# Attention, gate and phase mixer on one core: an exponential written ahead of each series of sines, one buffer ring for it and the convolution's product, and token products that wait for token weights alone

## The chip, the cores and the metric

The kernel runs on one core of a Trainium2 chip. The metric is the device time of one execution in microseconds. Times inside an execution come from a profile of one execution: TensorE (PE, with its weight loads PEld), VectorE (DVE), ScalarE (ACT), GpSimd (POOL) and the DMA queues, whose issuer here is SyncE (SP).

## The reference

Three layers in a row on four batches of 576 tokens with 8 heads of 64, so 512 channels. Setup makes some weights double precision words, which the kernel converts itself.

```python
scores = scale * np.matmul(q, k.transpose(0, 1, 3, 2))
kth = np.partition(scores, -32, axis=-1)[..., -32:-31]     # the 32nd largest of each row
attn = softmax(where(scores >= kth, scores, -1e9)) @ v
...
gate = sigmoid(sum(conv_w[k] * xp[:, k:k + S, :] for k in range(5)))   # causal, per channel
x = (gate * (x @ w_val)) @ w_out
...
theta = x @ w_theta
y = einsum('ts,bsd->btd', w_tok_r, x * cos(theta)) + einsum('ts,bsd->btd', w_tok_i, x * sin(theta))
u = x + y
out = u + np.maximum(u @ w_ch, 0.0)
```

## The kernel before, in words

Attention is cut into 144 tiles of 128 query rows by 576 keys (two heads of 64 rows share the short last tiles). The main loop at the end of `mixer` makes one step per tile and works on many tiles at once, in a software pipeline: in step i it issues the scores of tile i+3 on TensorE (`scores_pe`), copies those of tile i+2 out of PSUM on ScalarE (`scores_out`), finds candidates among the scores of tile i on VectorE (`pick`), compares and counts on ScalarE and POOL (`count`, `below`), takes the threshold of tile i-4 (`rest`, L621), writes the exponential of tile i-5 on ScalarE (`expo`) and masks tile i-6 with it on VectorE (`mask`, L674). Behind that TensorE transposes the masked tile (`turn`), ScalarE copies the transposes to SBUF as pT (`turn_out`), and TensorE multiplies them with v (`close`, px). The order of these calls within a step is written out by hand in `STEP` (in the first half of the loop `SOON`). VectorE and ScalarE run their instructions in exactly the order in which they are written; the other engines' queues are ordered by the framework's scheduler, by the order of writing where buffers and data allow.

The two layers behind the attention are "jobs", Python generators in the list `jobs`: for each batch `front(b)` (value product pval, output product px2t, angles pth, sines, the mixed values z) and `back(b)` (token products py, channel products ph, transposes and stores). Each step `work` lets the first job write some products, until the step's allowance of 4,150 ns (`BASE`, in some stages 6,000) less the cost of the step's attention is spent. Only the first job in the list runs; one that yields "sync" ends the step's work. A job's follow-up instructions on other engines are put into lists: `mid` runs at a fixed place in the next step, `later` at one behind it. The front of batch b+1 is put into `jobs` when the last tile of that batch's attention is closed. Batch 0's front comes in two halves (token tiles 0 and 1, then 2, 3 and the short tile 4), as its attention does.

The weights come as double precision words and are converted piece by piece by `cvt` on ScalarE, VectorE and POOL, half a piece a step, in the order conv, val, out, theta, tok, ch. `lacking[name]` counts the pieces that are still to be written. `want` then splits a channel weight into a high and a low half (`halve`: ScalarE casts, VectorE subtracts) and stores the halves in DRAM; the buffers of these halves are those of the conversion's raw pieces.

ScalarE reads its functions from tables. Sines have a table of their own; `tabled` orders sines against the functions Exp and Tanh, so that they don't alternate more than they are written. `trig` writes a batch's sines and cosines in two series (in batches 1 and 2 both in one long step, in which a drain of the jobs writes all the angles; in batch 3 after the last exponential).

Buffers: the exponentials have two buffers (tag "e" of pool `wk`). The convolution's tap on ScalarE, `ct` (L834), which POOL adds to the gate (L835), has one (tag "ct"); two helpers of the fallback and of the final check use it as well. The kernel has a second, exact version behind a flag (`safe`), which isn't entered with these inputs.

Of the kernel before, what the change touches and what calls it, by code (L numbers as in the profile page):

```python
# [11 lines left out]
F32 = mybir.dt.float32  # L12
# [78 lines left out]
def mixer(ctx, tc, qT, kT, vt, w_val, conv_t, w_out, w_theta, w_tok, w_ch, out, flag):  # L91
    nc = tc.nc
    safe = flag is None
    P = 128
    B, S, DM = vt.shape
# [15 lines left out]
    LAG = G + FLAG  # L111
# [6 lines left out]
    wk = ctx.enter_context(tc.tile_pool(name="wk", bufs=1))  # L118
# [34 lines left out]
    N = len(seq)  # L153
# [37 lines left out]
    taken, lacking = set(), {}  # L191
# [216 lines left out]
    def halve(hi, lo, src, key, also=None):  # L408

        def higher():  # L410
            nc.scalar.copy(hi, src)
            later.append(lower)

        def lower():
            engine(key).tensor_tensor(lo, src, hi.bitcast(F32), ALU.subtract)
            if also is not None:
                also()
            if PATIENT and attending[0]:
                later.append(lambda: done.add(key))
            else:  # L420
                done.add(key)

        mid.append(higher)
# [20 lines left out]
    def place(k, m):  # L444

        if k < 3 or k % 3 == 2:
            dt = F32R if k < 3 else I32
            both = []
            for t in ("hi", "lo"):
                if (t, m) in (("lo", 0), ("lo", 1)):  # L450
                    both.append(ml.tile([P, DM], dt, tag=f"{t}{m}", name=f"{t}{m}_{k}"))
                    continue
                pair = f"{t}{m - m % 2}{m - m % 2 + 1}"
                if (pair, k) not in places:
                    places[pair, k] = ml.tile([P, 2, DM], dt, tag=pair, name=f"{pair}_{k}")
                both.append(places[pair, k][:, m % 2, :])
            return both
        if (k, 0) not in places:
            names = ("val", "out") if k % 3 == 0 else ("theta", "ch")
            for t in range(2):  # L460
                places[k, t] = cp.tile([P, NC, DM], I32, tag=f"w_{names[t]}", name=f"w{t}_{k}")
        return [places[k, t][:, m, :] for t in range(2)]
# [3 lines left out]
    def want(b, name, last=NC - 1):  # L466

        k = PHASES.index((b, name)) if b else -1
        if k > 2:
            return  # L470
        for m in range(last + 1):
            if (b, name, m) in mats:
                continue
            src = W[name][:, m, :] if name == "theta" else W[name][:, :, m * P : (m + 1) * P]
            both = place(k, m)
            mats[b, name, m] = both
            stored[name, m] = dp.tile([P, 2, DM], I32, name=f"{name}{m}")

            def store(both=both, to=stored[name, m]):
                for t in range(2):  # L480
                    nc.sync.dma_start(to[:, t, :], both[t].bitcast(I32))

            hi, lo = (t if name == "theta" else t.rearrange("p (c w) -> p c w", c=NC) for t in both)
            halve(hi, lo, src, ("w", b, name, m), store)
# [27 lines left out]
    def after(*keys):  # L512
        while not done.issuperset(keys):
            yield "sync"
# [108 lines left out]
    def thr(i):  # L623
        at = N - 1 - i + NK - 1
        return thrs[:, at : at + 1]

    def nmax(g):

        d = groups[g]
        nc.gpsimd.tensor_scalar(least[:, g * G : g * G + G, :], d["tops"][:, :, 0 : KC : KC - 1], -1.0 / SMALL, None,  # L630
                                ALU.mult)

    def one_by_one(g):

        d = groups[g]
        spare = wk.tile([P, S], F32, tag="ct", name=f"spare_{g}")
        for k in range(G):
            src = s_tiles[g * G + k]
            for r in range(K // 8):
                top = d["tops"][:, k, 8 * r : 8 * r + 8]  # L640
                nc.vector.max(top, src)
                if r < K // 8 - 1:
                    nc.vector.match_replace(spare, top, src, LOWEST)
                    src = spare
            nc.vector.tensor_copy(thr(g * G + k), d["tops"][:, k, K - 1 : K])
        nmax(g)

    def check():

        bad = cp.tile([P, 3], F32, name="bad")  # L650
        worse = wk.tile([P, S], F32, tag="ct", name="worse")[:, :N]
        for j, (what, limit, op) in enumerate(((thrs[:, NK - 1 :], 2.0 ** -90, ALU.is_le),
                                               (thrs[:, NK - 1 :], 0.5, ALU.is_ge),
                                               (least[:, :, 1], -2.0 ** -60, ALU.is_ge))):
            nc.vector.tensor_scalar(worse, what, limit, None, op)
            nc.vector.tensor_reduce(bad[:, j : j + 1], worse, mybir.AxisListType.X, ALU.add)

        def on_pe(spare):
            nc.tensor.matmul(spare[:1, :3], ones, bad, start=True, stop=True)
            return lambda: nc.scalar.activation(said, spare[:1, :3], AF.Copy, accum_out=flag)  # L660
        extras.append((3, on_pe))

    def expo(i):
        e = seq[i]
        e.exp = wk.tile([P, S], F32, tag="e", name=f"e_{i}", bufs=2)
        tabled(e.exp, s_tiles[i], AF.Exp, bias=least[:, i, 0:1], scale=1.0 / SMALL)

    def mask(i):
# [52 lines left out]
    def close(part):  # L721

        u, x = part["u"], part["x"]
        b, hp = divmod(u, NP)
# [49 lines left out]
        for c in range(NF + 1):  # L774
            for j in (1, 0):
                d = slice(64 * j, 64 * j + 64)
                of_v, k = (v[:, c, d], j * NF + c) if c < NF else (v_last[:, d], 2 * NF)
# [23 lines left out]
        if split and x:  # L801
            g = gate[b][hp]
        else:
            drain(("gate", (u - GB) // NP))
            g = sp.tile([P, S], F32, tag="gp", name=f"gp_{u}", bufs=GB)
# [3 lines left out]
        g = g[:, lo:hi]  # L809
# [20 lines left out]
            return  # L830
        nc.scalar.activation(g, taps[0], AF.Copy, scale=cw[:, hp, 0:1])
        for k in CT:
            ct = wk.tile([P, S], F32, tag="ct", name=f"ct_{u}_{x}_{k}")[:, : g.shape[1]]
            nc.scalar.activation(ct, taps[k], AF.Copy, scale=cw[:, hp, k : k + 1])  # L834
            nc.gpsimd.tensor_tensor(g, g, ct, ALU.add)  # L835
            yield
            yield
# [15 lines left out]
    def front(b, xs):  # L853
# [79 lines left out]
        def angle(i):  # L933

            if late and i == NF:
                return sin_of(b, i)
            return gv[i % NF][:, :DM] if three else sin_of(b, i)
# [29 lines left out]
                nc.scalar.activation(g, h, AF.Abs)  # L967

        def trig(which):
            for i in which:  # L970
                f = angle(i)
                if i < NF:
                    g = cos_of(b, i)
                    tabled(g, g, AF.Sin, bias=half_pi, scale=-TURN)
                    tabled(sin_of(b, i), f, AF.Sin, scale=-TURN)
                else:
                    tabled(sin_of(b, i), f, AF.Sin, bias=trig_bias, scale=-TURN)
            if NF in which:
                gate.pop(b)
                done.add(("gate", b))  # L980
            later.append(lambda: done.update(("trig", b, i) for i in which))
# [117 lines left out]
    def back(b):  # L1099
        x2T = ms.pop(b)  # L1100

        def y_out(m, h, ps):
            lo, hi = COLS[h]

            def f():
                nc.vector.tensor_tensor(x2T[:, m, lo:hi], ps, x2T[:, m, lo:hi], ALU.add)
                if m == NC - 1 and (h or b == B - 1):
                    for k in (h,) if b == B - 1 else range(2):
                        halve_room(b, k, "U", x2T)
                if not h and m % 2:  # L1110
                    want(b, "ch", m)
            return f

        while any(lacking.values()):
            yield "sync"
        if b < B - 1:
            for h, m in [(h, m) for h in range(2) for m in range(NC)]:
# [57 lines left out]
        def turned(tiles):  # L1175
            for i in tiles:
# [4 lines left out]
                later.append(store(i, w, po))  # L1181
                yield 450

        for h, m in [(h, m) for h in range(2) for m in range(NC)]:
            lo, hi = COLS[h]
            yield from after(*halved(b, h, "U"), ("w", b, "ch", m))
            ps = ps_m.tile([P, hi - lo], F32, tag="m", name=f"ph_{b}_{m}_{h}")
            yield from products(ps, [(mat(b, "ch", m, c), chunk(b, h, "U", c)) for c in range(NC)])
            later.append(h_out(m, h, ps))
            if (h, m) == (1, NC - 1):  # L1190
                used(b, "ch")
            yield paid()
            if h and m == 1:
                yield from after(*[("o", b, c, 0) for c in range(NC)])
                yield from turned([0, 1])
# [9 lines left out]
    for b in range(B):  # L1205
        late = b == B - 1
        f = 1.275 if b in THREE else 1.675
# [53 lines left out]
    for k, part in enumerate(order):  # L1261
        i0 = part["tiles"][0].i
        u, x = part["u"], part["x"]
# [5 lines left out]
        elif split or x == 0:  # L1269
            when = (i0 - 7, i0 - 5, i0 - 5, i0 - 4, i0 - 3) if split or i0 and order[k - 1]["x"] and order[k - 1]["u"] // NP in SPLIT else (i0 - 9, i0 - 8, i0 - 7, i0 - 6, i0 - 3)  # L1270
            a = (u, x if split else None)
            for step, do in zip(when, (load_heads, split_high, split_low, *(
                    lambda u, x, j=j: double(u, j, x) for j in range(2)))):
# [28 lines left out]
        now, later[:] = list(later), []  # L1302
        run(now)

    begun = [0.0]

    def inside(i, f):
        if 0 <= i < N:
            f(i)
# [50 lines left out]
        "loads": lambda i: run(at_step.pop(i, [])),  # L1360
    }
    for i in range(N + LAG + TO + 12):
        for name in SOON if i < N // 2 else STEP:
            DO[name](i)
    attending[0] = False
# [52 lines left out]
```

## Time and profile before

| | |
|---|---|
| median of 3 runs | 833.06 us (832.63 to 834.16) |
| the profiled execution | 829.74 us |
| its span, first to last instruction | 827.9 us |
| mean granted clock of TensorE | 0.958 |
| busy: PE, DVE, ACT, POOL | 725.3, 669.0, 634.0, 451.7 us |

A row of a timeline gives start, duration, engine, line, operation and tiles, and in brackets how long the engine stood idle before the instruction and which instruction ended that. L674 is line 674 of the kernel before. A row of the waits gives who waited for whom, then total, times and longest in us.

### The profile page before, as it was taken

The numbers are of one execution on the slowest core, as the hardware profiler recorded it, in microseconds if no ns is written. First come the engines' busy times: TensorE is split into PE (matmuls) and PEld (weight loads), VectorE is DVE, ScalarE is ACT, GpSimd is POOL, SyncE is SP. The second block draws the span as 40 slices with busy tenths as digits, with TensorE's granted clock in tenths as the row PEclk, the third lists the DMA queues.
The fourth block names the chain that finished last, engine by engine and source line by source line (L and its number), as shares of the span: only waits on it lengthen the run. The fifth ranks groups of instructions, "written<-read, shape, count | busy, mean of one in ns | idle before, by whom it ended". The sixth has DMA issues, their size and how long they took to land.

```text
span 827.9 us, 15411 instructions
## 1 busy us (share of the span) xinstructions
PE 725.3 (88%) x4478; PEld 584.6 (71%) x4478; DVE 669.0 (81%) x2708; ACT 634.0 (77%) x1517; POOL 451.7 (55%) x557
## 2 busy tenths in 40 slices
PE   5467799958995799989889989999999899999995
PEld 3346577635754586778778767778988777898895
DVE  5999999879976979799899979989998695363522
ACT  6788999889769768788988988889987785346511
POOL 5976777446644554546687625647896252005500
PEclk9998999979997699989998999999999999999998
DMA  5676776545342225234855543234763200071002
GB/s 151 167 186 168 197 175 171 136 110 139 97 133 47 71 81 145 53 83 135 230 170 160 163 133 86 46 85 126 189 172 109 103 7 10 1 223 39 2 1 62
DMA packets 69985, 94.33 MB, mean 114 GB/s; under 512 B 13315, under 2 KB 36739, under 8 KB 69891
## 3 DMA queue, kind: packets, MB, share of 16 engines
q1 hardware_dynamic: 69568, 92.82, 41.2%
q8 instruction: 38, 0.62, 0.3%
q14 instruction: 59, 0.46, 0.2%
q10 hardware_dynamic: 320, 0.43, 0.2%
HBM read 49.96 MB, written 13.11 MB: 76 GB/s over the span
## 4 chain that ended last, share of the span: by engine, by line
PE 47%; DVE 27%; ACT 15%; POOL 4%; issue 3%; DMA 2%; SPq 1%; ACTq 0%; POOLq 0%; DVEq 0%
PE py L1127 9%; PE px L778 8%; DVE cand L594 5%; PE ph L529 4%; DVE s L674 4%; DVE thrs L621 4%; PE px2t L529 4%; PE pval L529 4%; PE pth L529 4%; PE pt L687 3%; PE py L1146 3%; PE ps L558 3%; ACT n L607 2%; DVE cand L600 2%; DVE gp L843 2%
## 5 line engine op out<-in xcount | busy, mean ns | idle before, releaser
L615 POOL TENSOR_TENSOR y<-s,n 128x576 f32<-128x576 f32 x144 | 188.9, 1312 | 205.0 <-DVE thrs L621 144.0
L594 DVE MAX8 cand<-s 128x8 f32<-128x96 f32 x864 | 210.5, 244 | 0.8 <-ACT s L572 0.6
L674 DVE SCALAR_TENSOR_TENSOR s<-s,thrs,e 128x576 f32<-128x576 f32 x144 | 137.8, 957 | 10.9 <-ACT e L202 10.9
L607 ACT ACTIVATE n<-s,tops 128x576 bf16<-128x576 f32 x144 | 112.1, 778 | 32.3 <-POOL y L615 11.3
L572 ACT ACTIVATE s<-ps 128x256 f32<-128x256 f32 (+1 forms) x288 | 103.7, 406 | 33.5 <-PE ps L691 11.5
L1127 PE MATMUL py<-w_tok,z 128*128 128x256 f32 (+1 forms) x432 | 115.0, 407 | 3.4 <-DVE z L986 3.4
L687 PE MATMUL pt<-ident,s 128*128 128x128 f32 x576 | 95.8, 290 | 25.3 <-ACT pT L706 17.3
L621 DVE MAX8 thrs<-y 128x8 f32<-128x584 f32 x144 | 109.3, 759 | 4.1 <-POOL y L616 3.6
L202 ACT ACTIVATE e<-s,least 128x576 f32<-128x576 f32 x144 | 110.8, 769 | 0.5 <-DVE s L674 0.4
L687 PEld LDWEIGHTS pt<-ident,s 128*128 128x128 f32 x576 | 70.5, 148 | 49.9 <-ACT pT L706 21.9
L558 PE MATMUL ps<-kh_None,q 128*128 128x256 f32 x240 | 93.7, 397 | 5.9 <-ACT s L572 3.9
L1127 PEld LDWEIGHTS py<-w_tok,z 128*128 128x128 f32 x432 | 77.8, 190 | 22.3 <-DVE z L986 5.0
L706 ACT COPY pT<-pt 128x512 f32<-128x512 f32 x128 | 73.2, 572 | 25.8 <-PE pt L687 15.6
L778 PE MATMUL px<-pT,v 128*64 128x256 f32 (+1 forms) x512 | 75.3, 430 | 17.3 <-ACT pT L706 17.3
L598 DVE MAX8 tops<-cand 128x8 f32<-128x48 f32 x432 | 82.8, 192 | 0.1
L559 PE MATMUL ps<-kl_None,q 128*128 128x256 f32 x240 | 72.5, 305 | 0.0
L778 PEld LDWEIGHTS px<-pT,v 128*64 128x64 f32 x512 | 34.1, 142 | 47.2 <-ACT pT L706 19.7
L558 PEld LDWEIGHTS ps<-kh_None,q 128*128 128x128 f32 x240 | 47.4, 198 | 22.2 <-ACT s L572 10.7
L600 DVE MATCH_REPLACE8 cand<-tops,cand 128x48 f32<-128x48 f32 x288 | 55.2, 192 | 0.0
L558 PE MATMUL ps<-kh,q 128*128 128x256 f32 (+1 forms) x80 | 36.0, 458 | 21.4 <-ACT s L572 9.3
L559 PEld LDWEIGHTS ps<-kl_None,q 128*128 128x128 f32 x240 | 48.1, 200 | 2.7 <-issue 0.5
L695 ACT COPY pT<-ps 64x128 f32<-64x128 f32 (+1 forms) x160 | 39.2, 245 | 11.5 <-PE ps L691 5.6
(206 smaller groups left out, 1726.9 us busy)
## 6 DMA issues: line engine op xcount, KB each, us to landing
kh_None<-kh_None SPq DMA_DIRECT2D x48, 144.0 KB, 2.7
kl_None<-kl_None SPq DMA_DIRECT2D x48, 144.0 KB, 2.7
v<-in_vt_dram SPq DMA_DIRECT2D x20, 256.0 KB, 3.3
out_dram<-x2T SPq DMA_DIRECT2D x16, 256.0 KB, 3.0
w<-ch SPq DMA_DIRECT2D x16, 256.0 KB, 4.6
w<-theta SPq DMA_DIRECT2D x16, 256.0 KB, 5.4
raw_hi<-in_w_tok_dram SPq DMA_DIRECT2D x7, 512.0 KB, 4.0
kh<-kh SPq DMA_DIRECT2D x24, 144.0 KB, 2.4
```

Of the source, the lines that this page charges most:

```text
L202: ins = nc.scalar.activation(out, src, func, **more).ins
L529: nc.tensor.matmul(ps[o : o + n], x, y, start=(i + k == 0), stop=(i == last and k == len(ways) - 1), skip_group_check=(n < P))
L558: nc.tensor.matmul(bank[:, :w], q2, kh[:, lo:hi], start=(j == js[0]), stop=False)
L559: nc.tensor.matmul(bank[:, :w], q2, kl[:, lo:hi], start=False, stop=(j == js[-1]))
L594: nc.vector.max(d["cand"][:, k, 8 * x : 8 * x + 8], s_tiles[i][:, x * SUB : (x + 1) * SUB])
L607: nc.scalar.activation(n, s_tiles[i], AF.Sign, bias=d["tops"][:, k, KC - 1 : KC], scale=-(1.0 + 2.0 ** -22), accum_out=acc)
L615: nc.gpsimd.tensor_tensor(y[:, :S], s_tiles[i], d.pop(("n", k)), ALU.mult)
L621: nc.vector.max(thrs[:, N - 1 - i : N - 1 - i + NK], d.pop(("y", k)))
L674: nc.vector.scalar_tensor_tensor(p, p, thr(i), e.exp, ALU.is_ge, ALU.mult, accum_out=part["sums"][:, e.slot : e.slot + 1])
L687: nc.tensor.transpose(e.pt[:, c, :], p[:, c * P : (c + 1) * P], ident)
L778: nc.tensor.matmul(px[d, :], of_v, pT[:, k, :], start=(c == 0), stop=(c == NF), skip_group_check=True)
L1127: nc.tensor.matmul(ps, z[:, m * P : (m + 1) * P], W["tok"][:, w, lo:hi], start=(i + k == 0), stop=(i == NF))
```

## The change

Three edits. `expo` returns if the tile's exponential is already written, and `trig` calls it first, for the exponential that the next step would write (`step[0]` holds the loop's step). The tag "ct" is gone: the convolution's tap and the two helpers take buffers of tag "e", which now has three. `back` waits only for the token weights before the products py, and for the channel weights ahead of the products ph; the splits of channel weights that fall due before the last of these is converted are held in the list `due`.

```diff
@@ one_by_one, check: the same for spare and worse
-        spare = wk.tile([P, S], F32, tag="ct", name=f"spare_{g}")
+        spare = wk.tile([P, S], F32, tag="e", name=f"spare_{g}", bufs=3)
...
     def expo(i):
         e = seq[i]
-        e.exp = wk.tile([P, S], F32, tag="e", name=f"e_{i}", bufs=2)
+        if hasattr(e, "exp"):
+            return
+        e.exp = wk.tile([P, S], F32, tag="e", name=f"e_{i}", bufs=3)
         tabled(e.exp, s_tiles[i], AF.Exp, bias=least[:, i, 0:1], scale=1.0 / SMALL)
...
         for k in CT:
-            ct = wk.tile([P, S], F32, tag="ct", name=f"ct_{u}_{x}_{k}")[:, : g.shape[1]]
+            ct = wk.tile([P, S], F32, tag="e", name=f"ct_{u}_{x}_{k}", bufs=3)[:, : g.shape[1]]
...
         def trig(which):
+            if not safe:
+                inside(step[0] - LAG + 2, expo)
             for i in which:
...
-                if not h and m % 2:
-                    want(b, "ch", m)
+                if not h:
+                    due.append(m)
+                    while due and m % 2 and not lacking["ch"]:
+                        want(b, "ch", due.pop(0))
             return f

-        while any(lacking.values()):
+        due = []
+        while lacking["tok"]:
             yield "sync"
...
+        while lacking["ch"]:
+            yield "sync"
+        while due:
+            want(b, "ch", due.pop(0))
         for h, m in [(h, m) for h in range(2) for m in range(NC)]:
             lo, hi = COLS[h]
             yield from after(*halved(b, h, "U"), ("w", b, "ch", m))
...
-    begun = [0.0]
+    begun, step = [0.0], [0]
...
     for i in range(N + LAG + TO + 12):
+        step[0] = i
         for name in SOON if i < N // 2 else STEP:
```

## Rows read from the trace of the kernel before

**Rows 1.** The page, engines: busy us, share of the span, instructions.

```profile
PE 725.3 (88%) x4478; PEld 584.6 (71%) x4478; DVE 669.0 (81%) x2708; ACT 634.0 (77%) x1517; POOL 451.7 (55%) x557
```

**Rows 2.** VectorE's waits, whole span: us in total, times, longest.

```profile
DVE s L674 <- ACT e L202: 10.9, 3, 5.6
```

**Rows 3.** ScalarE's timeline, batch 0's second series of sines and after it.

```profile
255.06 1.28 ACT L202 ACT_TABLE_LOAD   x1
...
261.26 1.28 ACT L202 ACT_TABLE_LOAD   x1
262.56 0.77 ACT L202 ACTIVATE e<-s,least 128x576 f32<-128x576 f32 x1
263.24 0.57 ACT L706 COPY pT<-pt 128x512 f32<-128x512 f32 x1
...
277.75 0.76 ACT L202 ACTIVATE e<-s,least 128x576 f32<-128x576 f32 x1
```

**Rows 4.** VectorE's timeline in the same stretch.

```profile
257.41 0.40 DVE L340 TENSOR_SCALAR tmp<-tmp 128x512 f32<-128x512 f32 x1
263.37 0.82 DVE L674 SCALAR_TENSOR_TENSOR s<-s,thrs,e 128x576 f32<-128x576 f32 x1 [5.56 <-ACT e L202]
...
264.45 2.48 DVE L986 TENSOR_TENSOR z<-px,z 128x512 f32<-128x512 f32 x4
...
271.60 2.44 DVE L843 SCALAR_TENSOR_TENSOR gp<-xT,w_conv,gp 128x576 f32<-128x576 f32 x2
...
281.97 0.82 DVE L674 SCALAR_TENSOR_TENSOR s<-s,thrs,e 128x576 f32<-128x576 f32 x1
```

**Rows 5.** TensorE's timeline in the same stretch.

```profile
263.86 1.12 PE L687 MATMUL pt<-ident,s 128*128 128x128 f32 x4 [7.85 <-ACT pT L706]
...
286.25 4.05 PE L1127 MATMUL py<-w_tok,z 128*128 128x256 f32 x18
```

**Rows 6.** Instructions on tiles w_tok, w_ch: ns min/median/max, first to last start.

```profile
L354 POOL TENSOR_TENSOR w_tok<-raw_lo x4: 746/1492/1494, 145.2 to 229.6; 128x512 int32<-128x512 int32 x3, 128x64 int32<-128x64 int32 x1
...
L354 POOL TENSOR_TENSOR w_ch<-raw_hi x3: 1485/1487/1494, 242.6 to 282.2; 128x512 int32<-128x512 int32 x3
```

**Rows 7.** Stretches: length, busy PE, PEld, DVE, ACT, POOL; clock, DMA share, GB/s.

```profile
254.00:286.00 32.00, 17.32 (x87) 11.66 (x84) 26.41 (x101) 26.65 (x59) 18.03 (x20) 0.63 0.24 52
286.00:348.00 62.00, 59.99 (x347) 47.01 (x347) 52.71 (x243) 45.97 (x115) 29.90 (x37) 1.00 0.34 94
348.00:395.00 47.00, 40.96 (x286) 35.39 (x284) 44.56 (x183) 40.74 (x100) 28.72 (x36) 0.93 0.46 121
```

**Rows 8.** VectorE's waits from 286 to 395.

```profile
DVE x2T L1106 <- PE py L1127: 8.1, 4, 3.3
...
DVE x2T L1158 <- PE ph L529: 1.1, 1, 1.1
```

**Rows 9.** Groups by line: count, busy us, mean ns, idle before and its releaser.

```profile
L1127 PE MATMUL py<-w_tok,z 128*128 128x256 f32 (+1 forms) x432 | 115.0, 407 | 3.4 <-DVE z L986 3.4
...
L202 ACT ACT_TABLE_LOAD x9 | 11.5, 1283 | 0.2
```

**Rows 10.** POOL's timeline, batch 0's second series.

```profile
268.99 1.41 POOL L835 TENSOR_TENSOR gp<-gp,ct 128x576 f32<-128x576 f32 x1
```

**Rows 11.** Timelines of ScalarE and VectorE, batch 0's first series of sines.

```profile
172.64 0.42 ACT L202 ACTIVATE gp<-pconv 128x320 f32<-128x320 f32 x1
...
172.76 0.82 DVE L674 SCALAR_TENSOR_TENSOR s<-s,thrs,e 128x576 f32<-128x576 f32 x1 [4.48 <-ACT e L202]
```

**Rows 12.** Timelines of VectorE and TensorE, batch 1's sines and what follows.

```profile
479.17 0.69 DVE L950 SCALAR_TENSOR_TENSOR gp<-gp,pth 128x512 f32<-128x512 f32 x1 [4.10 <-ACT gp L943]
...
495.72 0.48 PE L1127 MATMUL py<-w_tok,z 128*128 128x256 f32 x1 [0.59 <-DVE z L986]
```

**Rows 13.** VectorE's timeline at 341.79; L621 alone from 286 to 348, busy, count.

```profile
341.79 0.49 DVE L1106 TENSOR_TENSOR x2T<-py,x2T 128x320 f32<-128x320 f32 x1 [3.34 <-PE py L1127]
...
286.00:348.00 62.00, 10.48 (x14) 1.00 0.34 94
```

More of the change, by code (lines that the diff above doesn't have):

```diff
@@ L650, in check @@
         bad = cp.tile([P, 3], F32, name="bad")
-        worse = wk.tile([P, S], F32, tag="ct", name="worse")[:, :N]
+        worse = wk.tile([P, S], F32, tag="e", name="worse", bufs=3)[:, :N]
         for j, (what, limit, op) in enumerate(((thrs[:, NK - 1 :], 2.0 ** -90, ALU.is_le),
```

## The prediction

> **What bounds the kernel now.** I read the page first: TensorE is busy 88% and VectorE 81% of the span [rows 1], so neither sets the time by its sum, and a change has to be read in its own stage. Then VectorE's waits over the whole span: the masking step (L674) waits only three times for ScalarE's exponential, 10.9 us in all [rows 2]. Then the timelines around the longest of these. In batch 0's second series of sines ScalarE loads the sine table at 255.06, loads the exponential's table at 261.26 and writes the next exponential at 262.56 [rows 3]. By then VectorE has stood still for 5.56 us [rows 4], and TensorE for 7.85, because its transposes need a bank that ScalarE's copy pT empties only from 263.24 [rows 3, 5].
>
> Next the weights. The token weights are whole at about 231, the channel weights only at 283.7 (282.2 + 1.49) [rows 6], and the first token product py starts at 286.25 [rows 5]. The values z that it reads are written by 267 for four of batch 0's five token tiles [rows 4]. So the products wait some 19 us for weights that they don't read.
>
> Last the stretches. From 254 to 286 TensorE is busy 17.3 of 32 us, at a mean granted clock of 0.63, so much of it at 1.2 GHz after standing idle; VectorE is busy 26.4. From 286 to 348, where batch 0's token products run, TensorE is busy 60.0 of 62 at full clock, VectorE 52.7. From 348 to 395, with U's halves and the channel products, VectorE leads with 44.6 of 47 [rows 7]. An empty stretch of TensorE, one where TensorE sets the pace, one where VectorE does. VectorE's idle time in the last two is 9.3 + 2.4 = 11.7 us; 8.1 of it are four waits of the addition x2T (L1106) for a product py, 1.1 one for a channel product [rows 8].
>
> **The change, part by part.**
>
> The exponential ahead of the sines. There are as many exponentials and as many table loads (9 [rows 9]) as before. The next step's exponential moves from behind the sines to ahead of them, and the load of its table moves on to the next user of that table.
>
> In batch 0's second series the sines come one exponential, 0.77 us [rows 3], later. Behind them the load and the exponential, 1.28 + 0.77 = 2.05, leave the way, so pT and what follows up to the next exponential come 1.28 earlier. VectorE's mask at 263.37 can follow its previous instruction, which ended at 257.8 [rows 4]. What is late next: the multiplications z wait for the sines, the next candidates for scores that ScalarE copies behind pT; then the convolution's sum (L843, 271.60) waits for POOL's (L835), which started at 268.99 [rows 4, 10] behind ct. The table load now stands between pT and ct, so ct is as late as before; POOL's sum, which also waited for another job of POOL's, can start perhaps 1 us earlier, at 267.9, and ends 1.41 later, at 269.3. So VectorE keeps 271.6 - 269.3 = 2.3 of its 5.56 us, and TensorE and ScalarE keep 1.28. I take 1.3, since TensorE sets the pace behind it; bounds 0 and 5.6.
>
> In batch 0's first series the gate's Tanh stands right behind the exponential and reads the same table, so the load stays, and so does pT behind it. VectorE could mask 4.48 us earlier [rows 11], but the scores two tiles on hang on that same chain. I take 0; bounds 0 and 4.5.
>
> In batches 1 and 2 no mask waits long (5.56 and 4.48 are both batch 0's; 0.9 is left for the third). There the exponential only delays the sines by 0.77, in a chain in which VectorE already waits 4.10 us for ScalarE; behind it TensorE waits 0.59 for the last z [rows 12], which takes most of the delay up. So 0.2 each, +0.4 in all; bounds 0 and 1.5.
>
> The Trainium skill, "ScalarE: Activation LUTs", section "What ACT_TABLE_LOAD costs", prices a switch of tables at about 2.66 us, load and drain. Here the load takes 1.28 and the exponential begins 1.30 after it [rows 3], so the trace shows no such drain. By the page's price pT would come about 1.4 us earlier still, and the sum below would be larger by as much; I keep the trace's.
>
> The shared buffers. An exponential had two buffers, ct one. With three for both, ct takes the buffer of the exponential two tiles back, which the exponential just ahead of it on ScalarE had to wait for until now. So 0; if a ct is held up, POOL's sum is late, by at most one mask (0.82 [rows 4]) for each of 12: bound +9.8 at the very worst, and nearer 0, since ScalarE waits at present for no such buffer.
>
> Token products earlier. Nothing is added to any engine. The products can start one step after the sines, near 266, and all but the first few behind the last z, near 272. The planner lets 4,150 ns a step through, the attention's share included. From 286 to 348 that put 115.0/3 = 38.3 us of products [rows 9] into 14 steps (14 thresholds [rows 13]), 2.7 us a step; four steps earlier means some 11 us of products ahead of before. They can't stay ahead: batch 1's front is queued when batch 1's attention is done, which products don't hasten. So four steps without products come back behind batch 0's channel products, near 380 to 395, and the gain is what VectorE's idle time shrinks by: at most 11.7, at least 0.
>
> What part of it? In the first ten product steps TensorE stays the later engine: they begin with steps of much VectorE work (7.5 us from mask 263.37) but on a slow clock, so I expect those waits to stay. The last four steps of the old stretch lose their products. The longest wait for a py, 3.34 us, lies there, at 341.79 [rows 13], and goes; the one for the channel product, 1.1 [rows 8], too: 4.4 us. The channel weights' halves are written four together instead of two and two, some ten steps before their use: 0, bounded by the same idle time.
>
> The sum: -1.3 + 0.4 - 4.4 = -5.3 us. The profiled execution took 829.74 us (span 827.9), so 824.4 for such a one. The median of the timed runs is 833.06, which is 3.3 above it; against that the prediction is 833.06 - 5.3 = **827.8 us**.
>
> **The rivals.**
>
> All of it: the products fill the heavy steps, no idle time of VectorE is left up to 395: -11.7 - 1.3 = -13.0, 820.1. For it: TensorE has 32 - 17.3 = 14.7 us empty before 286 [rows 7]. Against it: the waits arise where attention's own products and py meet in one step, which can happen anywhere.
>
> Given back: the four empty steps come again behind the channel products, TensorE idles there, the four waits only move, and the exponential's gain is lost in waits for TensorE. For it: the work is the same and batch 1's front doesn't move; against it: the longest wait lies where no product is left. 0 to -1.6, so 831.5 to 833.1.
>
> Slower, by a cold start: the products begin at 1.2 GHz, where the 18 that took 4.05 us at 286.25 [rows 5] take 8.1. In TensorE's order the next tile's scores stand behind them, in ScalarE's the next exponential behind the copy of those scores. If the clock stays low through two product steps of 2.7 + 0.6 us, that costs 6.6 us more. The slack to it: the exponential of 277.75, done at 278.5, was used by the mask of 281.97 [rows 3, 4], 3.5 us. The rest, 3.1, is lost, less the channel product's 1.1: +2.0, 835.1. It decides once the extra time passes 3.5 us. For it: the clock of 0.63 before 286; against it: with products TensorE has no gap there, and the full clock came before with the first gapless work [rows 7].
> The Trainium skill, "TensorE: Matmul & The Clock Gate", section "What's actually happening", says that throttled is the default and activity releases it. By that rule the early products would themselves raise the clock, and this rival is the less likely; the trace agrees so far, with 0.63 in the idle stretch and 1.00 in the next [rows 7].
>
> **How the numbers follow.** Partial gain, as summed: 0.50 (own range 825 to 830.5). All of it: 0.18. Given back: 0.18. Slower: 0.14. A difference within 0.2%, 1.7 us, can't be told from none on this kernel. Faster is the first two, 0.68; the same 0.18; slower 0.14. The range leaves out the far end of "all of it" and the part of "slower" past its own sum (where held-up buffers lie too): 821.0 to 834.6.
>
> **What would show it.** Right: the waits of L674 for L202 fall from 10.9 to under 2 us; the first py starts between 264 and 270; the granted clock from 254 to 286 is above 0.75; the waits of x2T for py up to 395 fall from 8.1 to about 5; and from batch 1's first products on the two traces run in parallel, 4 to 6 us apart. Wrong: new waits of VectorE on ScalarE's scores or exponentials between 270 and 290 (cold start); a stretch near 380 to 395 as long as before (given back); POOL waiting longer for ct (buffers).

## The result and the profile after

The changed kernel takes **818.38 us** in the median of 4 runs (817.32 to 819.17); beside it the kernel before took 832.85 (829.89 to 834.16). The ratio is 0.983, interval 0.980 to 0.986: 1.7% faster, which is more than the predicted range allowed. The profiled executions are 11.0 us apart (829.74 and 818.77), the medians 14.5. The places below come from the profiles; the 3.5 us between these two differences are taken up with the profiles of the kernel before, at the end of the experiments.

Line numbers have moved: the mask is L676 now (L674 before), pT L708, z L990, the addition x2T L1110, py L1134, POOL's convolution sum L837.

First the page, engines (busy us, share of the span, count) and the mask's group (its last part is the idle time before the masks):

```profile
PE 722.8 (88%) x4478; PEld 580.9 (71%) x4478; DVE 665.9 (82%) x2708; ACT 633.6 (78%) x1517; POOL 451.4 (55%) x557
L676 DVE SCALAR_TENSOR_TENSOR s<-s,thrs,e 128x576 f32<-128x576 f32 x144 | 140.8, 978 | 2.3 <-ACT e L202 2.3
```

The work is that of [rows 1]; the idle time before the masks is 2.3 us where it was 10.9 [rows 2].

ScalarE's timeline at batch 0's second series of sines, which answers to [rows 3]:

```profile
254.09 0.81 ACT L202 ACTIVATE e<-s,least 128x576 f32<-128x576 f32 x1
254.92 1.28 ACT L202 ACT_TABLE_LOAD   x1
256.21 0.72 ACT L202 ACTIVATE z<-z,half_pi 128x512 f32<-128x512 f32 x1
...
261.01 0.57 ACT L708 COPY pT<-pt 128x512 f32<-128x512 f32 x1
...
263.68 1.28 ACT L202 ACT_TABLE_LOAD   x1
264.98 0.78 ACT L202 ACTIVATE e<-s,least 128x576 f32<-128x576 f32 x1
```

The exponential stands ahead of the sines, and pT follows them without a table load between: 261.01, where it was 263.24. The load comes one exponential later.

VectorE's timeline, which answers to [rows 4]:

```profile
168.57 2.48 DVE L990 TENSOR_TENSOR z<-px,z 128x512 f32<-128x512 f32 x4
...
256.93 0.81 DVE L676 SCALAR_TENSOR_TENSOR s<-s,thrs,e 128x576 f32<-128x576 f32 x1
...
258.00 2.47 DVE L990 TENSOR_TENSOR z<-px,z 128x512 f32<-128x512 f32 x4
...
265.79 0.82 DVE L676 SCALAR_TENSOR_TENSOR s<-s,thrs,e 128x576 f32<-128x576 f32 x1 [0.99 <-ACT e L202]
...
268.61 1.67 DVE L845 SCALAR_TENSOR_TENSOR gp<-xT,w_conv,gp 128x576 f32<-128x576 f32 x2 [2.00 <-POOL gp L837]
```

The mask that stood at 263.37 behind 5.56 us of waiting is at 256.93 with no wait, 6.4 us earlier. The next one waits 0.99 for its exponential, and the convolution's sum 2.00 for POOL's, as the prediction's "what is late next" had it. At the mask of 285.10 before, 282.01 after, 3.1 us are left; the trace was 0.8 ahead before this series (most of it from a DMA near 148), so 2.3 belong to the exponential.

TensorE's timeline, which answers to [rows 5]:

```profile
255.04 1.89 PE L1134 MATMUL py<-w_tok,z 128*128 128x256 f32 x8
258.74 3.52 PE L1134 MATMUL py<-w_tok,z 128*128 128x256 f32 x14 [1.81 <-DVE z L990]
262.09 0.60 PE L689 MATMUL pt<-ident,s 128*128 128x128 f32 x4
262.53 0.60 PE L1134 MATMUL py<-w_tok,z 128*128 128x256 f32 x2
...
263.60 4.48 PE L1134 MATMUL py<-w_tok,z 128*128 128x256 f32 x20
```

The first py is at 255.04, not at 286.25, and not near 266 either: the products run while ScalarE still writes sines, in the time in which TensorE stood idle for 7.85 us. They stand ahead of the transposes pt in the queue that the scheduler ordered. The first 8 records read the values z of token tiles 0 and 1, which VectorE had written from 168.57 on; the next 14 wait for those of tiles 2 and 3, written from 258.00 on.

The windows of after: the stretch of [rows 7] first (length, busy PE, PEld, DVE, ACT, POOL, clock, DMA share, GB/s), then py alone (length, busy PE with the number of records, clock, DMA share, GB/s), in three parts and in the whole stretch:

```profile
254.00:286.00 32.00, 27.78 (x160) 21.80 (x160) 27.67 (x116) 28.90 (x64) 17.93 (x22) 1.00 0.32 75
...
254.00:264.00 10.00, 6.40 (x26) 1.00 0.23 49
264.00:275.00 11.00, 7.00 (x29) 1.00 0.20 42
275.00:286.00 11.00, 4.22 (x18) 1.00 0.53 132
...
254.00:286.00 32.00, 17.61 (x72) 1.00 0.32 75
```

TensorE is busy 27.8 of 32 us where it was 17.3, at full clock where it was 0.63. Half of batch 0's token products, 72 of 144 records, are begun by 286 (a record that crosses a boundary counts in both parts); before, none was.

VectorE's waits in after from 254 to 395 (total, times, longest), which answers to [rows 8]:

```profile
DVE gp L845 <- POOL gp L837: 6.8, 2, 4.9
DVE lo_-1_3823 L415 <- ACT hi_-1_3822 L411: 1.7, 1, 1.7
DVE cand L594 <- ACT s L572: 1.3, 1, 1.3
DVE s L676 <- ACT e L202: 1.0, 1, 1.0
DVE thrs L621 <- POOL y L616: 0.9, 1, 0.9
```

No x2T waits for a py any more (8.1 us before), nor for a channel product (1.1). But the first row holds a wait of 4.9 us that before had not. VectorE's and POOL's timelines there:

```profile
387.61 1.67 DVE L845 SCALAR_TENSOR_TENSOR gp<-xT,w_conv,gp 128x576 f32<-128x576 f32 x2 [4.85 <-POOL gp L837]
```

```profile
379.54 1.55 POOL L415 TENSOR_TENSOR X<-xT,X 128x256 fp32r<-128x256 f32 x2
...
382.13 1.33 POOL L415 TENSOR_TENSOR X<-xT,X 128x320 fp32r<-128x320 f32 x1
...
384.78 1.27 POOL L615 TENSOR_TENSOR y<-s,n 128x576 f32<-128x576 f32 x1
386.02 0.20 POOL L616 TENSOR_TENSOR y<-steps,acc 128x8 f32<-128x8 f32 x1
386.18 1.40 POOL L837 TENSOR_TENSOR gp<-gp,ct 128x576 f32<-128x576 f32 x1
```

POOL makes a row of X's splits (L415), and the convolution's sum gp stands behind them. My reading is that the jobs now reach batch 1's front early enough that what it still needs falls due in one step; the experiment that takes the row apart tests it.

Following the masks, counted from the first: after is ahead by 3.1 us at the 56th (285.10 before), 7.5 at the 64th (324.26), 10.7 at the 72nd, 13.5 at the 80th (395.41 against 381.94), 10.4 at the 81st, behind that wait, and between 9.8 and 12.0 from there on; 11.0 at the last.

### The profile page after: what moved, and what is told of

It is laid out like the page before. It is cut to its first block, busy times and chain, and to the rows that moved or that the text cites. A ratio compares the mean times of both kernels' runs of the same rounds, so it can differ in the third digit from the quotient of the medians.

```text
span 817.0 us, 15416 instructions
## 1 busy us (share of the span) xinstructions
PE 722.8 (88%) x4478; PEld 580.9 (71%) x4478; DVE 665.9 (82%) x2708; ACT 633.6 (78%) x1517; POOL 451.4 (55%) x557
## 4 chain that ended last, share of the span: by engine, by line
PE 43%; DVE 30%; ACT 13%; POOL 6%; DMA 4%; issue 3%; SPq 1%; ACTq 0%; POOLq 0%; DVEq 0%
PE px L780 7%; PE py L1134 7%; DVE cand L594 6%; DVE s L676 5%; DVE thrs L621 4%; PE pval L529 4%; PE px2t L529 4%; PE pth L529 4%; PE ph L529 4%; PE py L1153 3%; PE pt L689 3%; DVE gp L845 2%; DVE cand L600 2%; PE ps L558 2%; DVE tops L598 2%
## 5 line engine op out<-in xcount | busy, mean ns | idle before, releaser
L676 DVE SCALAR_TENSOR_TENSOR s<-s,thrs,e 128x576 f32<-128x576 f32 x144 | 140.8, 978 | 2.3 <-ACT e L202 2.3
L607 ACT ACTIVATE n<-s,tops 128x576 bf16<-128x576 f32 x144 | 112.0, 778 | 32.0 <-POOL y L615 13.5
L1134 PE MATMUL py<-w_tok,z 128*128 128x256 f32 (+1 forms) x432 | 116.1, 408 | 6.4 <-DVE z L990 6.4
L621 DVE MAX8 thrs<-y 128x8 f32<-128x584 f32 x144 | 109.3, 759 | 5.4 <-POOL y L616 4.8
L202 ACT ACTIVATE e<-s,least 128x576 f32<-128x576 f32 x144 | 110.8, 769 | 1.4 <-POOL gp L837 1.3
L558 PE MATMUL ps<-kh_None,q 128*128 128x256 f32 x240 | 91.9, 390 | 5.5 <-ACT rb L759 2.8
L1134 PEld LDWEIGHTS py<-w_tok,z 128*128 128x128 f32 x432 | 77.4, 190 | 26.4 <-DVE z L990 8.8
L708 ACT COPY pT<-pt 128x512 f32<-128x512 f32 x128 | 73.1, 571 | 23.2 <-PE pt L689 13.5
```

Of the source, the lines that this page charges most:

```text
L202: ins = nc.scalar.activation(out, src, func, **more).ins
L558: nc.tensor.matmul(bank[:, :w], q2, kh[:, lo:hi], start=(j == js[0]), stop=False)
L607: nc.scalar.activation(n, s_tiles[i], AF.Sign, bias=d["tops"][:, k, KC - 1 : KC], scale=-(1.0 + 2.0 ** -22), accum_out=acc)
L621: nc.vector.max(thrs[:, N - 1 - i : N - 1 - i + NK], d.pop(("y", k)))
L676: nc.vector.scalar_tensor_tensor(p, p, thr(i), e.exp, ALU.is_ge, ALU.mult, accum_out=part["sums"][:, e.slot : e.slot + 1])
L1134: nc.tensor.matmul(ps, z[:, m * P : (m + 1) * P], W["tok"][:, w, lo:hi], start=(i + k == 0), stop=(i == NF))
```

## The experiments

Each kernel was measured beside the kernel before on the same chip. For the products alone, the exponential with the buffers, the products one step later and the splits taken apart, that took 832.66 us (828.41 to 835.99, 14 runs); for after once more, the old buffers, the buffers alone and the earlier front 832.83 (17 runs); for the unread work 834.37 (13 runs).

**The products' edit alone.** The edits of `back` are kept, those of `expo`, `trig` and the buffers undone:

```diff
-        if hasattr(e, "exp"):
-            return
-        e.exp = wk.tile([P, S], F32, tag="e", name=f"e_{i}", bufs=3)
+        e.exp = wk.tile([P, S], F32, tag="e", name=f"e_{i}", bufs=2)
...
-            if not safe:
-                inside(step[0] - LAG + 2, expo)
...
```

> The products' edit alone: the token products wait for token weights only, the exponentials and buffers stay as in the kernel before. Theory 1 (the hole): TensorE's order lets the products run ahead of transposes that still wait, so they fill the time in which ScalarE writes the sines; first product near 255, granted clock of 254 to 286 at 0.95 or more, and 8 to 10 us of the 14.5 come from here: 823 to 825 us. Rival (both needed): without the exponential ahead VectorE still stands 5.6 us at the mask and the values z come late, so the products gain only what was predicted, 4.4: 828 to 829.

Measured: 823.72 us (823.03 to 826.15), ratio 0.990 (0.987 to 0.993); its profile is 6.7 ahead at the last mask. TensorE's timeline:

```profile
255.76 1.89 PE L1130 MATMUL py<-w_tok,z 128*128 128x256 f32 x8
...
263.76 1.11 PE L687 MATMUL pt<-ident,s 128*128 128x128 f32 x4 [6.12 <-ACT pT L706]
```

The products start as early as in after, but only 8 records fit in ahead of the transposes: VectorE writes the next z behind the mask that still waits 5.5 us for its exponential. By the 56th mask 54 records are done (64 in after). That is enough to take the waits of x2T for py up to 395 from 8.1 to 1.0 us. So the edit of `back` is worth 8.9 us by itself in the medians, 6.7 between the profiles, where the prediction's term for it was 4.4. The granted clock from 254 to 286 is 0.89 and not the 0.95 or more that was expected.

**The exponential ahead and the buffers, products as before.** The edits of `back` are undone:

```diff
-        while lacking["tok"]:
+        while any(lacking.values()):
             yield "sync"
...
```

> The exponential ahead of the sines and the three shared buffers alone; the products wait for all weights as before. Theory 1: the two long waits of the mask go, the first is given back to ScalarE's scores, the second leaves 2.3 us at VectorE: 830 to 831.5 us, with the product stretch unchanged. Rival: VectorE keeps all of the second wait: 827.

Measured: 826.66 us (825.27 to 831.49, 9 runs), ratio 0.995 (0.992 to 0.998). In the profile the kernel is 3.4 us ahead at the 56th mask, of which 0.4 stood before the sines, and then flat: 3.6 at the 67th, 3.8 at the 80th and at the last. VectorE keeps what it gained at the sines and gets nothing more; x2T still waits 7.7 us for py. By the medians it is 6.0, which is the time that the rival had; the trace has theory 1's mechanism, with about 3 us kept at the sines. This sum and that of the products alone, 6.0 + 8.9 = 14.9, make up the whole change's 14.

**The products one step later.** After, but batch 0's first token product waits for all five of its z instead of the first half's:

```diff
-                yield from after(*[("z", b, i) for i in SETS[0]])
+                yield from after(*[("z", b, i) for i in SETS[0] + SETS[1] * (b == 0)])
```

> The changed kernel, but batch 0's first token product waits until the values z of all five token tiles are written in the planner's order, one step later. Theory 1 (the hole): TensorE stands idle again from 255 to about 262, its clock falls to 1.2 GHz in 254 to 286, and 4 to 6 us are given back: 822.5 to 824.5. Rival (steps): the gain comes from products being some three steps ahead of the old order, and one step less costs at most 1 us: 818 to 819.5.

Measured: 823.73 us (822.34 to 825.36), ratio 0.989 (0.986 to 0.992), so 5 of the 14 us are given back by one step. Its windows, columns as for after (all engines; then py alone, in the three parts up to 286):

```profile
254.00:286.00 32.00, 26.00 (x140) 19.70 (x140) 27.67 (x116) 28.94 (x65) 18.53 (x22) 0.89 0.30 67
...
254.00:264.00 10.00, 6.19 (x19) 0.83 0.14 30
264.00:275.00 11.00, 4.52 (x18) 1.00 0.28 59
275.00:286.00 11.00, 3.04 (x14) 0.84 0.48 108
```

And a row of VectorE's timeline:

```profile
305.31 0.49 DVE L1110 TENSOR_TENSOR x2T<-py,x2T 128x320 f32<-128x320 f32 x1 [2.53 <-PE py L1134]
```

The products still begin inside TensorE's empty time (256.01, where this trace runs 1.0 behind that of after), so the step it loses is not the one at the sines, where the expectation had it, but one of those behind: 50 records by 286 instead of 72. Then TensorE is late again: x2T waits 3.7 us for py, and two other waits of VectorE for ScalarE, 2.0 and 1.9, are new. The granted clock is 0.83 and 0.84 in two of the parts, so TensorE ran at half of full speed in some of each. Whether the clock or the missing work costs the 5 us this run can't tell; the next can.

**TensorE kept busy with work that nobody reads.** The kernel just described, and 22 products more (44 records) ahead of batch 0's first token product, whose result is unused:

```diff
+        if b == 0:
+            ps = ps_m.tile([P, 256], F32, tag="m", name="warm")
+            for k in range(22):
+                nc.tensor.matmul(ps, cos_of(0, k % 2)[:, :P], W["tok"][:, k % 2, :256], start=(k == 0), stop=(k == 21))
```

> The kernel whose first token product waits for all values z (823.7 us in the first call), with 22 products in the same place whose result nothing reads: they keep TensorE at work in the hole, but bring no token product forward. Theory 1a (the clock is what the hole is worth): TensorE's granted clock stays at full speed and the time comes back to the changed kernel's, 818 to 820. Theory 1b (the work is what it is worth): the clock stays up, the 22 products still have to be done later, and the time stays at 822.5 to 825.

Measured: 825.12 us (823.53 to 827.32, 8 runs), ratio 0.990 (0.987 to 0.993). Its windows from 254 to 286 (all engines; then py alone, in three parts):

```profile
254.00:286.00 32.00, 31.52 (x184) 26.58 (x184) 27.66 (x116) 28.91 (x65) 18.48 (x22) 1.00 0.30 66
...
254.00:264.00 10.00, 0.00 (x0) 1.00 0.13 28
264.00:275.00 11.00, 5.88 (x24) 1.00 0.29 61
275.00:286.00 11.00, 5.97 (x28) 1.00 0.46 105
```

The clock is full throughout, and no time comes back: up to the 80th mask this trace keeps within 0.5 us of the one without the extra products. It also shows that it doesn't matter when within the stretch the products run: here they begin at 266.65 instead of 256.01, are 50 by 286 as there, and x2T waits for py the same 3.7 us. What counts is how many are done before the steps in which TensorE sets the pace. The test covers the clock between 0.89 and 1.00 only: no run has the 0.63 of before beside a full clock with the same products.

**The row of splits taken apart.** After, but batch 1's splits for the second token half are made one by one, each behind a value product of the first half:

```diff
-                split_x(b, c, x)
+                if not (x and b == 1):
+                    split_x(b, c, x)
...
             later.append(val_out(m, x, ps))
+            if b == 1 and not x:
+                split_x(b, m, 1)
```

> The changed kernel, but batch 1's splits of the second half of X are written one by one behind the first half's value products instead of all eight splits in one step. In the changed kernel VectorE waits 4.85 us for POOL's convolution sum at 387.6, which stands behind POOL's row of splits. If that row is the cause, the wait goes and 3 to 4.5 us come off: 814 to 815.5. Rival: the value products of the second half then wait for their splits and VectorE waits for them instead: 818 to 819.

Measured: 816.59 us in the median of five executions (815.85 to 818.96), ratio 0.982 (0.978 to 0.985), less of a gain than the 814 to 815.5 expected. POOL's timeline at the same place, and VectorE's waits from 254 to 395:

```profile
385.64 1.28 POOL L615 TENSOR_TENSOR y<-s,n 128x576 f32<-128x576 f32 x1 [0.95 <-DVE thrs L621]
386.87 0.20 POOL L616 TENSOR_TENSOR y<-steps,acc 128x8 f32<-128x8 f32 x1
387.03 2.20 POOL L415 TENSOR_TENSOR X<-xT,X 128x320 fp32r<-128x320 f32 x2
```

```profile
DVE gp L845 <- POOL gp L837: 2.0, 1, 2.0
DVE lo_-1_3823 L415 <- ACT hi_-1_3822 L411: 1.7, 1, 1.7
```

The wait of 4.85 us is gone, and the 81st mask is 15.0 us ahead of before (10.4 in after). Of these 4.6 us about 2.3 are left at the last mask (13.3 ahead against 11.0), and 2.1 in the medians (818.7, the mean of the two medians of after, less 816.59); the intervals of the ratios overlap, so that it is the trace that shows it. So the row of splits gave back part of the gain. This version has the lowest median of all, but a sixth execution of it took 3761 us and is not in these numbers; no trace of it exists and its cause stays open, so the version serves here as evidence and not as a proposal.

**After once more, and after with the old buffers.** The first is the changed kernel itself; the second has two buffers for the exponentials and one of its own for ct:

```diff
-        e.exp = wk.tile([P, S], F32, tag="e", name=f"e_{i}", bufs=3)
+        e.exp = wk.tile([P, S], F32, tag="e", name=f"e_{i}", bufs=2)
...
-            ct = wk.tile([P, S], F32, tag="e", name=f"ct_{u}_{x}_{k}", bufs=3)[:, : g.shape[1]]
+            ct = wk.tile([P, S], F32, tag="ct", name=f"ct_{u}_{x}_{k}")[:, : g.shape[1]]
...
```

> The changed kernel itself, once more beside the others of this call. Both theories: 818 to 819 us; its waits of VectorE between 254 and 395 as in its first profile.

> The changed kernel with the old buffers: two for the exponentials, one of its own for the convolution's product. Theory 1: the exponential ahead needs no third buffer, since the mask that frees its buffer is done by then, so within 1 us of the changed kernel: 817.5 to 819.5. Rival: the exponential ahead waits for a mask, the sines behind it as well, and 2 us or more are lost: above 820.5.

Measured: 819.07 (818.63 to 820.22) and 818.81 (818.47 to 820.25), both at a ratio of 0.984 (0.981 to 0.986). In the whole change the buffers are worth nothing either way. The second profile of after says something of the clock as well:

```profile
254.00:286.00 32.00, 29.13 (x165) 23.34 (x161) 27.68 (x116) 28.91 (x65) 18.46 (x22) 0.95 0.30 65
```

The clock is 0.95 here instead of 1.00; the same 72 records are begun by 286, no x2T waits for a py, and the profiled execution took 818.63 us as against 818.77.

**The buffers alone.** The kernel before with the three shared buffers, nothing else:

```diff
-        e.exp = wk.tile([P, S], F32, tag="e", name=f"e_{i}", bufs=2)
+        e.exp = wk.tile([P, S], F32, tag="e", name=f"e_{i}", bufs=3)
...
```

> The kernel before with three buffers shared by the exponentials and the convolution's product, and nothing else. Theory 1 (the buffers do nothing by themselves): within 1.7 us of the kernel before, about 832.7. Rival (the looser exponentials give ScalarE freedom): 1.7 us faster or more, below 831.

Measured: 829.88 us (827.52 to 834.24, 12 runs), ratio 0.997 (0.995 to 0.999). So the time is the rival's, 2.95 us below that of before with the interval below 1, but the profile shows no place for it: this trace is mostly 0 to 1.4 us ahead of that of before, with no lasting step at an exponential or a ct. It would account for the median of the kernel with exponential and buffers gaining more than its profile: 6.0 less these 3.0 is the 3 that the trace shows. Why the buffers help by themselves and not in the whole change stays open.

**Batch 1's front queued earlier.** The version with the splits taken apart, and batch 1's jobs enter the list once the first half of its last part is closed:

```diff
         if not split and x == 0:
+            if b == 1 and hp == NP - 1:
+                jobs.append(front(b, (0, 1)))
+                jobs.append(back(b))
             return
...
```

> The kernel with the spread splits of the first call, and batch 1's front queued as soon as the first half of its last part is closed, so that three quarters of the first half's value products can run in the steps between 365 and 382 that have no products now. Theory 1 (what ends the gain is that batch 1's front can't start): about 4 us of products move into them, TensorE's idle time there shrinks, and 2 to 4 us come off the spread kernel's 817: 813 to 815. Rival (the rest is bound by VectorE): 816 to 817.5.

Measured: 819.24 us (817.77 to 820.44), ratio 0.983 (0.980 to 0.985), 2.65 us more than the median without it and more than either theory had. A failed idea: against the version without it the trace falls back by 2.6 us between the 56th and the 80th mask, and it wins nothing behind that.

**The kernel before, three more profiles.** They were taken to see what makes its executions differ.

> The kernel before, profiled again. Its timed runs spread over 7 us, those of the changed kernel over 2. Theory 1 (the empty stretch): the spread comes from TensorE's clock, which falls to 1.2 GHz in the stretch from 254 to 286 and comes back at a different place in each execution; a slower execution then differs from the first profile there by 2 to 4 us. Rival: the spread comes from elsewhere (the first 50 us, the last stretch), and the change removes it by chance or not at all.

> As the run before it: a further execution of the kernel before, to see where two executions differ. Theory 1: between 254 and 286. Rival: elsewhere.

> As the two runs before it. Theory 1: between 254 and 286. Rival: elsewhere.

Measured: 828.28, 829.1 and 835.61 us. I had suspected that the slower executions lose their time in TensorE's empty stretch, which after no longer has. Most of that falls. The stretch in the slowest profile:

```profile
254.00:286.00 32.00, 17.31 (x79) 10.90 (x78) 26.40 (x99) 26.65 (x59) 18.03 (x20) 0.63 0.23 49
```

It is the stretch of [rows 7] within 0.1 us on every engine but the weight loads. But one piece of the loss does come from there. The same products px and the first addition x2T behind them, in the first profile of before and then in the slowest:

```profile
281.56 2.31 PE L778 MATMUL px<-pT,v 128*64 128x256 f32 x12
290.34 0.42 DVE L1106 TENSOR_TENSOR x2T<-py,x2T 128x256 f32<-128x256 f32 x1 [1.04 <-PE py L1127]
```

```profile
282.10 2.83 PE L778 MATMUL px<-pT,v 128*64 128x256 f32 x12
291.75 0.42 DVE L1106 TENSOR_TENSOR x2T<-py,x2T 128x256 f32<-128x256 f32 x1 [1.92 <-PE py L1127]
```

In the slowest execution the half clock lasts further into the work (granted 0.52 in the 3.54 us from 282.10, as against 0.77 in the 3.54 from 281.56), TensorE has no gap from there to its first py, and x2T waits 0.9 longer for it; the masks behind stay 0.9 further back. That is 0.9 us where 2 to 4 were expected. The rest of the 6.0 us that this execution lies behind the first profile at the last mask gathers in pieces of 0.4 to 1.3 us, some of them given back, between the 36th and the 132nd mask; what makes them is not known. So the profile of before shown in front is one of the quicker ones of a kernel that runs from 828 to 836 us, while after runs from 817 to 820; that is the 3 us between the two differences.

## Why the prediction was wrong

The forecast was 827.8 us, the median is 818.38: 9.4 apart. Between the profiles 11.0 us were gained and 5.3 forecast, so 5.7 of the 9.4 are a matter of mechanism. The other 3.7 come from the last line of the sum, which carried the 3.3 us between the profile and the median of before over to after; after has no such distance (818.77 and 818.38).

**The exponential.** Right in mechanism: the wait goes, the next waits are those named, and VectorE keeps 2.3 us, the figure worked out. I entered 1.3, on the argument that TensorE sets the pace behind it. The kernel with the exponential and the buffers alone keeps 3.0 us in its trace (3.4 less the 0.4 that stood before), through the whole stretch in which TensorE sets the pace, so the argument fails even without early products. The first series is worth 0 to 0.2, as said, and the trace has no loss at the sines of batches 1 and 2 beyond 0.7 us (0.4 was entered).

**The buffers.** Nothing in the whole change, as said; alone 3.0 by medians against the 0 expected, unexplained.

**The table load.** The step by the trace's 1.28 us was the right one: in after the load begins at 254.92 and the first sine at 256.21, 1.29 later. So the 2.66 us that the Trainium skill, "ScalarE: Activation LUTs", section "What ACT_TABLE_LOAD costs", gives for a switch is again not what this queue shows.

**The products: the step that failed.** It is the term under "What part of it?", 4.4 us; measured are 8.9 alone and 8.0 on top of the exponential by the medians (826.66 less 818.7), 6.7 and 7.2 between the profiles. Two of its premises were wrong.

The first was "some 11 us of products ahead". By 286 after has done 72 records, and at [rows 9]'s 115.0/432 = 0.27 us each that is 19 us (17.6 by the rows of after). I let the first of them start near 266, one step after the sines, and most of them behind the last z. But the z of token tiles 0 and 1 had been whole since the first series of sines (171 in after), and in TensorE's queue products that are ready pass the transposes that wait for ScalarE, so the first of them run at 255, and 48 are begun before the last z is written (270.95 in after). The next z come early as well, at 258.00 instead of 264.45, since they stand behind the mask that no longer waits. That makes five steps ahead of 286 instead of four, with 3.8 us of products each instead of 2.7.

The second was "on a slow clock, so I expect those waits to stay". The clock was granted in full, and the waits of x2T for py went entirely. The kernels with the products one step later and with the unread work decide which of the two mattered more: raising the clock from 0.89 to 1.00 brings nothing, a step's products fewer costs 5 us. Begun by the 56th mask are 0 records before, 40 with the unread work, 43 with the products one step later, 54 with the products alone and 64 in after; of the waits of x2T for py up to 395 there remain 8.1, 3.7, 3.7, 1.0 and 0 us. The clock of the stretch doesn't order them so: 0.63, 1.00, 0.89, 0.89 and 1.00 (0.95 in the second profile of after). So enough head start empties the stretch in which TensorE sets the pace. The slow clock of before did have a part in the first of the waits, 1.04 us, as the slowest profile's 1.92 shows.

**The rivals.** "All of it" described what happened up to the 80th mask: VectorE's idle time goes, 13.0 us by its sum, 13.5 - 0.8 = 12.7 in the trace. The argument against it, that waits arise wherever attention's products and py meet, fails where py is ahead. "Given back" came true in another way than I had it: not by TensorE standing idle in steps without products, but by 3 us at POOL's row of splits, which I had not looked for. "Cold start" is refuted: full clock, and between 254 and 395 no new wait on scores longer than 1.3 us. As the prediction put it, the Trainium skill, "TensorE: Matmul & The Clock Gate", section "What's actually happening", has activity release the throttle; the early products ran at 1.00 where the same stretch had 0.63.

**The signs to look for.** The wait of L674 for L202, "under 2 us": 2.3 in all, right but for 0.3. First py "between 264 and 270": wrong, 255. Clock "above 0.75": right. Waits of x2T for py "to about 5": wrong, 0. Traces "4 to 6 us apart" from batch 1's products on: parallel, but 10 to 12 apart. Short steps came back behind the channel products, three of them, with the masks 3.1 to 3.4 us apart from 363.7 to 373.2 and VectorE busy throughout.

## What to carry to other kernels

Where a scheduler orders an engine's queue, read from the data's readiness and not from the order of writing when an instruction can start: an instruction ready early passes one that waits. An idle stretch of an engine ahead of one in which it sets the pace is worth the work that can be moved into it, counted in instructions done before that stretch begins; the moment within it didn't matter here, and its clock only where it was still low when the next stretch began (0.9 us). And where work ends earlier, look for the next producer whose jobs now fall due together, and what stands behind them in the same queue.

## What was not expected of the hardware

The kernel before spreads over 8 us from execution to execution (828 to 836 in three sets of 13 to 17 runs), in many small pieces of which only one, 0.9 us, comes out of the stretch that the change empties; after spreads over 3. The two other kernels without early products spread over 6 to 7 us (9 and 12 runs), the six others with them over 2 to 4 (5 to 8 runs), so the spread seems to go with the products; by what way no run shows. And of the 23.9 us at half clock, which begin within 4 us of one another in all four profiles of before (at 259.3 in the first), the one cost that a trace shows is in the wait behind their end. What they cost in all stays open: no run has before's products at a full clock there.
